# Pairing tiles in PSUM banks and re-ordering the work of an attention-plus-MLP kernel

## The chip, the cores and the metric

The kernel runs on one core of one Trainium2 chip. The metric is the device time of one execution in microseconds (us). The kernel before takes 694.83 us, the median of three runs that lie between 694.37 and 696.42 us.

## The reference

The input `x` has 2048 tokens of 512 numbers. It is normalised token by token, and the result feeds two branches that are added to `x`: causal attention in segments with a compressive memory, and a two-layer MLP. All weights and results are fp32.

```python
x = A_x
xn = _layernorm(x, axis=-1)
return x + _A_ref(xn, A_wq, A_wk, A_wv, A_wo, A_beta) + _B_ref(xn, B_w1, B_b1, B_w2, B_b2)
```

The attention has 32 heads of 16 numbers and 4 segments of 512 tokens. Inside a segment it is an ordinary causal softmax; the memory `M`, `z` carries the earlier segments:

```python
logits = jnp.einsum("bhqd,bhkd->bhqk", qs, ks) * scale + mask
p = _softmax(logits, axis=-1)
a_dot = jnp.einsum("bhqk,bhkd->bhqd", p, vs)
num = jnp.einsum("bhld,bhde->bhle", pq, M)
o = g * a_mem + (1.0 - g) * a_dot
M = M + jnp.einsum("bhld,bhle->bhde", pk, vs)
```

The MLP normalises `xn` again, multiplies by `w1` (512 by 1792), adds a bias, takes a GELU, multiplies by `w2` (1792 by 512) and adds a second bias.

## The kernel before

**Units.** The attention is cut into 16 units, one for each segment and each group of 8 heads. The MLP is cut into 16 units of 256 tokens and 7 of the 14 hidden blocks of 128 (FH = 7).

**Jobs.** The program is a list of small jobs; the letters in quotes are their keys in `streams()` and `CALL`. For TensorE they are of three kinds, by how they use its array of 128 by 128 cells:

- Full array, 128 rows and 128 columns, in `split3` (L480) and `out_jobs` (L815): the query and key projections "T" and the value projection "V" (12 matmuls of 512 columns, since each fp32 product is made of three fp16 products over four slices of 128), the first MLP layer "D" (12 matmuls of 256 columns for one hidden block), and the output projection "out".
- Two halves of 64 rows that work side by side: the maxima "M" (L621), the scores "S" (L661), the second MLP layer "e" (L797, 14 parts of 6 matmuls for one MLP unit), small transposes (L499) and the memory's denominator "Qd" (L571).
- Four column strips of 32 columns side by side, in fp32: the weighted sums of the values "pv" and "PV" (L690, four parts kb = 0 to 3 of 8 instructions each) and the memory update "K" (L602).

**One attention unit.** "T" projects queries and keys, splits them into two fp16 halves and sends them through DRAM into stacked layouts, `kst` and `qst`. "M" multiplies queries by keys for one of four head places t on both halves of the array, and VectorE takes the row maxima under the causal mask (L628). "R" transposes the maxima and sends them through DRAM into two extra rows of `qst`. "S" multiplies the other way round, so that keys lie on partitions and the maximum is already taken off; ScalarE takes the exponential (L666) and GpSimd clears the half above the diagonal (L675). "pv" adds up the values with those weights, for the head places 0 and 2 (half h = 0) and then 1 and 3 (h = 1). "O" divides by the sums.

**The four key blocks.** Causality makes the score strips of key block kb 512, 384, 256 and 128 queries long (`LEN`). For one t, "S" has three jobs: kb 0 (512 columns), kb 1 and 3 together (512) and kb 2 (256). Each job takes two PSUM banks, one for each half of the array, and gives two exponentials. The results lie in a buffer `pt` of 1280 columns, at `OFF`, of which there are 4. "M" has three jobs for one t: query block 3 (512 columns), blocks 2 and 0 (384 and 128) and block 1 (256).

**One MLP unit.** "D" fills 256 columns of a bank for one hidden block, and VectorE scales them into `hz` (L756). "G" takes the seven GELUs on ScalarE (L763), "H" splits the result into two fp16 halves (L770 to L772 on GpSimd and ScalarE), and "e" multiplies by `w2`.

**What sets the order.** Two strings. Each letter of `ORDER` takes the next job of one of 28 streams, and the jobs' instructions go to the five engines in that order; every engine keeps its own order. `BANKS` names the PSUM bank, 0 to 7, for every call of `dense()`, one after the other. Nothing is decided on the chip. The first part of the program also loads, squares ("wm", L311) and splits ("ws", L366 to L371) the six weight matrices; some pieces wait in buffers that later hold other things (`stage`). "warm" is a filler of 8 matmuls.

Of the kernel before, what the change touches and what calls it, by code (L numbers as in the profile page):

```python
# [9 lines left out]
F32 = mybir.dt.float32  # L10
# [9 lines left out]
P = 128  # L20
D = 512
# [25 lines left out]
OFF = [0, 512, 1024, 896]  # L47
# [9 lines left out]
def streams():  # L57
    keys, queries, nat, maxi, soft, vals_p, heads, memo, vals, norm, again, hid, act, mlp, outs, accs, wts = (
        [] for _ in range(17))
    for i in range(NU):  # L60
# [3 lines left out]
        maxi += [("M", i, n) for n in range(12)] + [("R", i)]  # L64
# [17 lines left out]
    for j in range(NU):  # L82
        hf, fh = divmod(j, 2)
        hid += [("D", j, f) for f in range(FH)]
# [18 lines left out]
    "aatcucuccvavtctveecttcetcuvaactvuvtaatcattavdtubcwwvccfwxxcxwxyxyxxgyhxcoxxvwxofooowcvwzyzoiyyiazgyyziiynzoiiys"  # L103
    "ppAnziiniicvzvcniiooAzmAihiiopzqqiqcivpqjpqjijqqijizqjiqqjiiAwszBzoAskkkkmjiAojoijsoAijAqjqjasAfoAopgkkkkpjpjqq"
    "jlpoolojjjooilihAAkkkkpaiqqiqijqjqqijqjiqjqjisBfgpiiqkkkkmpliqqiooiqpBlqoBopohijjiojiijpolsjiqaqajqiqiqqiiqapka"
    "kmkktspaqijqiqjqiqajqbqajopijjgBfopkkkBkjjjlooooBlhjjjolqiqqiipkkkkjiqqijqqjjiqiqjjqiqiqiBkkkkmpliilfnplimpngrr"
    "mrjjponijqjqjinjipiskmkkmkaiijrijjoojiqsjqqjiqiiiqqkkkkihlqlfmlogojqjqjqqjjasoojmkkkkmqjiqjqjjaojjpipmooisikkkk"
    "lpilhiofmgoooqiqpppqiqiqqqiiiqqpsosmoiqqiiqiqppsslooijqjojijojijoiaakkkkmpaijqjqjaqqqjiqqjiqjqiikmkkakbqiaqqahl"
    "olfqjjojqmjgjjoolmmkkkkmhjjoojjiitjiojiippkkkkliiilnfnimpligniinipmrrijjrsijqjqiqjiqjqiipkmkkksiqjqijqjqjiqjqii"
    "qjqikmpkkkiprlqsphlfojmjgopjjlojpjoomokmkkkqiqisjojiqisjqiqijqqijqhiqqiiqjsqiiqppmkkkkilalofomqpgopaoooospmlajq"  # L110
    "qqjqqjqjqiiqiqqqjqiqqipipooooiijooppoiaakkkkmajiqpisqqjiqjqjaiqaqhjqqqjqaaqmkkkkbjlfoljqjmjgojjqolmkkkkmmjjjooj"
    "jioijoiiippkpkkkiinliifniiilnnimlgrpmjjrmjjjrrijikkpskkiqqijqiqijqqjiqjiqjqiqjiqiispqkpkskksqilqoplfojmjgjjjpoo"
    "oojolmkkkkiqjiqpsjiqiqijqjqiqijqjiqiqiqiiqqkksmkpikplolfjjqmjgjjjoooooklpkmkkjiiopjqiqijqjiqpjqiqijqiqqiqiiqikk"
    "pspkkqiplpoooopljjjqqqjqjjqooolkpskmkpkmqqqpqjpjqqqjqjqpqqjqjqqqkmkkkqlllqqqqqqqqqrrrr"
# [5 lines left out]
    "012345670123457063571265407321640573216405732164053271640527163054271630542713605427105472105427105472105472015"  # L120
    "470251407251405712470512470512470536124075631254076340125637123756123576132576132576132576132576135402761350427"
    "163054273106542736574326574326537425632754632574631072456310724563071245360712453620731620731067203617621073621"
    "073621073621037621037621037261702361475023671540263701524603175246031746013746013713460713471630471630463714067"
    "314056723410523674105236741052367410527410527410527410527410527140352671450326475103264751023674523674523647253"
    "647236547236475264735264107532410765324107265431067512043675120436751204736152047361520473615270346150312750317"
    "250317253107250371257013275027135027134650132754062751340621375460376054370567403056374065374065307645307645307"
# [21 lines left out]
def infini_mixer_kernel(ctx: ExitStack, tc: tile.TileContext, x, wq, wk, wv, wo, beta, w1, b1, w2, b2, out):  # L148
# [69 lines left out]
    def col(j):  # L218
        return sc[:, j:j + 1]
# [21 lines left out]

    def four(t):
        return t.rearrange("p (k c) -> p k c", k=KT)

    def w_load(m, k):
        if m in ("qk", "QK"):
            g = 0 if m == "qk" else 1 + k
# [663 lines left out]
```

## Time and profile before

| What | Value |
|---|---|
| Median of three runs | 694.83 us |
| Profiled execution, first to last instruction (span) | 693.1 us |
| Median less span | 1.7 us |
| TensorE clock granted, mean | 0.995 |
| TensorE with a matmul in it | 678.7 us |
| VectorE, ScalarE, GpSimd busy | 535.4, 522.7, 347.2 us |
| Moved by DMA | 55.12 MB |

The profile holds one execution. The profiled execution's own time is its span of 693.1 us; the runs' time also holds what lies around the span, 1.7 us by the difference to the median. PE is TensorE's matmul side and PEld its weight loads, DVE is VectorE, ACT ScalarE, POOL GpSimd and SP the queue that starts the transfers. Lines such as L480 are lines of the kernel before. A group's row gives its busy time in us and the mean length of one instruction in ns; where instructions overlap, busy time over count is less than that mean. A busy PE need not be PE at its peak, because matmuls are pipelined.

### The profile page before, as it was taken

What the parts mean: (1) busy time and instruction counts of PE and PEld (TensorE: products, weight loads), DVE (VectorE), ACT (ScalarE), POOL (GpSimd) and SP (SyncE); (2) the same over time, 40 slices, a digit from 0 to 9 for tenths busy, and PEclk for the clock granted to TensorE, in tenths of its full rate; (3) what the DMA queues carried; (4) which work ended last, traced back from release to release, by engine and by line L of the source; (5) the groups of instructions that cost most, each with busy time, mean ns of one, the idle gap of its engine ahead of it and who ended that gap; (6) DMA issues with size and microseconds to landing.
All of it is one profiled execution on the core that took longest, in us unless ns stands there. A gap on an engine that the chain in (4) does not pass through costs nothing.

```text
span 693.1 us, 16949 instructions
## 1 busy us (share of the span) xinstructions
PE 678.7 (98%) x6359; PEld 395.7 (57%) x6359; DVE 535.4 (77%) x1695; ACT 522.7 (75%) x1013; POOL 347.2 (50%) x533
## 2 busy tenths in 40 slices
PE   7799999999999999999999999999999999999997
PEld 6465556576654555566554456567564456656653
DVE  4499978897795887998798786888678595969442
ACT  5989898878795659857795697757795687778870
POOL 5276768365624425664334445454362546455752
PEclk9899999999999999999999999999999999999999
DMA  9984222420204213431113224231120416140101
GB/s 272 283 238 136 64 63 63 108 62 14 84 10 115 87 44 74 100 71 33 51 45 92 63 72 99 63 93 33 31 80 24 132 18 152 18 108 3 18 1 61
DMA packets 51790, 55.12 MB, mean 80 GB/s; under 512 B 4782, under 2 KB 40636, under 8 KB 51708
## 3 DMA queue, kind: packets, MB, share of 16 engines
q1 hardware_dynamic: 49404, 49.84, 25.3%
q0 software_dynamic: 2304, 4.20, 3.7%
q8 instruction: 50, 0.82, 0.5%
q14 instruction: 32, 0.26, 0.1%
HBM read 36.99 MB, written 17.04 MB: 78 GB/s over the span
## 4 chain that ended last, share of the span: by engine, by line
PE 78%; ACT 10%; POOL 4%; DVE 3%; issue 2%; DMA 1%; SPq 1%; POOLq 0%; ACTq 0%; DVEq 0%
PE ps L480 33%; PE ps L797 16%; PE ps L690 10%; PE ps L815 6%; PE ps L661 5%; PE ps L621 5%; ACT pt L666 2%; DVE ps L628 2%; PE ps L571 2%; PE ps L499 1%; ACT hT L763 1%; ACT hT L771 1%; SPq L252 1%; POOL w1s L371 1%; DMA pt<-in_A_wk_dram 1%
## 5 line engine op out<-in xcount | busy, mean ns | idle before, releaser
L628 DVE CUSTOM_DVE_ANT_0 ps<-ps,mask 128x512 f32<-128x512 f32 (+3 forms) x512 | 233.8, 522 | 16.1 <-PE ps L621 14.9
L666 ACT ACTIVATE pt<-ps,qkcs 128x512 f32<-128x512 f32 (+1 forms) x384 | 206.1, 624 | 35.3 <-PE ps L661 33.5
L797 PE MATMUL ps<-w2s,hT 64*128 64x512 f16 x1344 | 176.7, 376 | 0.2
L480 PE MATMUL ps<-xnT,w1s 128*128 128x256 f16 x1344 | 157.8, 273 | 0.0
L675 POOL TENSOR_SCALAR_AFFINE_SELECT pt<-pt 128x256 f32<-128x256 f32 x256 | 99.1, 414 | 92.0 <-ACT pt L666 91.0
L480 PEld LDWEIGHTS <-w1s 128*128 128x128 f16 x1344 | 127.3, 98 | 29.1 <-issue 11.3
L772 POOL TENSOR_TENSOR hT<-hh,hT 128x512 f16<-128x512 f32 x64 | 67.8, 1059 | 82.8 <-ACT hT L771 81.0
L797 PEld LDWEIGHTS <-hT 64*128 64x128 f16 x1344 | 76.3, 94 | 50.7 <-issue 6.0
L690 PE MATMUL ps<-pt,vt 128*32 128x512 f32 (+3 forms) x1024 | 77.3, 435 | 0.1
L756 DVE SCALAR_TENSOR_TENSOR hT<-ps,sc,sr 128x256 f32<-128x256 f32 x112 | 52.1, 478 | 27.2 <-PE ps L480 27.0
L628 DVE DVE_READ_ACCUMULATOR2_ANT mc<- 128x1 f32 x512 | 70.6, 138 | 0.0
L661 PE MATMUL ps<-qst,kst 50*128 50x512 f16 (+3 forms) x512 | 67.5, 298 | 0.3 <-ACT pt L666 0.2
L621 PE MATMUL ps<-kst,qst 48*128 48x256 f16 (+3 forms) x512 | 67.1, 297 | 0.5
L771 ACT ACTIVATE hT<-hh 128x512 f16<-128x512 f32 x64 | 36.6, 572 | 33.4 <-POOL hh L770 32.9
L690 PEld LDWEIGHTS ps<-pt,vt 128*32 128x32 f32 x1024 | 31.3, 109 | 42.4 <-issue 30.8
L770 POOL TENSOR_SCALAR hh<-hT,sc 128x512 f32<-128x512 f32 x64 | 41.8, 653 | 26.6 <-ACT hT L763 24.9
L720 POOL TENSOR_TENSOR nN<-nN,oT 128x512 f32<-128x512 f32 x16 | 20.3, 1267 | 61.3 <-DVE oT L546 61.3
L763 ACT ACTIVATE hT<-hT,b1t 128x256 f32<-128x256 f32 x112 | 46.4, 495 | 0.2
L480 PE MATMUL ps<-xnT,wqs 128*128 128x512 f16 x192 | 45.6, 389 | 0.0
L480 PE MATMUL ps<-xnT,wks 128*128 128x512 f16 x192 | 44.3, 379 | 0.0
L480 PE MATMUL ps<-wvs,xnT 128*128 128x512 f16 x192 | 44.0, 380 | 0.1
L815 PE MATMUL ps<-wos,oT 128*128 128x512 f16 x192 | 43.2, 380 | 0.6 <-POOL oT L726 0.6
(217 smaller groups left out, 890.0 us busy)
## 6 DMA issues: line engine op xcount, KB each, us to landing
kd<-hl SPq DMA_DIRECT2D x48, 128.0 KB
qd<-hl SPq DMA_DIRECT2D x48, 128.0 KB
kst<-kd SPq DMA_DIRECT2D x32, 192.0 KB
qst<-qd SPq DMA_DIRECT2D x32, 192.0 KB
acc<-in_A_x_dram SPq DMA_DIRECT2D x16, 256.0 KB
acc<-in_B_b_dram POOLq DMA_DIRECT2D x16, 256.0 KB, 4.1
out_dram<-acc SPq DMA_DIRECT2D x16, 256.0 KB
xt<-in_A_x_dram SPq DMA_DIRECT2D x14, 256.0 KB
```

Of the source, the lines that this page charges most:

```text
L480: T.matmul(p, wsl(ws, k, a), xsl(xs, k, b), start=s0 and i == 0, stop=s1 and i == 3 * n - 1)
L621: T.matmul(p[:, o:o + n], stk[i, 0][r, t, P * qb:P * qb + P], stk[i, 1][r, t, :n], start=True, stop=True)
L628: V.tensor_tensor_reduce(p[:, o:o + n], p[:, o:o + n], mask[:, 512 - n:], 1.0, -3e38, OP.add, OP.max, mc[:, 16 * b + 4 * t + qb:16 * b + 4 ...
L661: T.matmul(p[:, o:o + n], stk[i, 1][r, t, P * kb:P * kb + P], stk[i, 0][r, t, P * kb:], start=True, stop=True)
L666: A.activation(e[:, OFF[kbs[0]]:OFF[kbs[0]] + o], p[:, :o], AF.Exp, scale=qkcs[:, 1, i % NG:i % NG + 1])
L675: G.affine_select(v, v, pattern=[[0, 2], [1, P]], compare_op=OP.is_ge, fill=0.0, base=0, channel_multiplier=-1)
L690: T.matmul(p[32 * c:32 * c + 32, P * kb:], vt[s, kb][:, 4 * g + c, 16 * odd:16 * odd + 32], pt[i, 2 * c + odd][:, OFF[kb]:OFF[kb] + LEN[kb ...
L756: V.scalar_tensor_tensor(hz[:, fi, :], p[:, :256], col(F1 + fh), srow[hs][:, own], op0=OP.mult, op1=OP.mult)
L763: A.activation(z, z, AF.Gelu_apprx_tanh, bias=b1t[:, FH * (j % 2) + f:FH * (j % 2) + f + 1])
L772: G.tensor_tensor(hT[:, z, 1, :], t, hT[:, z, 0, :], op=OP.subtract)
L797: w = T.matmul(pes[j][a], hTs[fh][r, fi, u, P * a:P * a + P], w2s[r, fo, v, :], start=n == 0 and m == 0, stop=fi == FH - 1 and m == 2, ski ...
L815: T.matmul(p, o[:, u, P * b:P * b + P], wos[:, g, v, :], start=i == 0, stop=i == 3 * NG - 1)
```

## The change

Four things are changed.

- "D" takes two hidden blocks at a time: they fill the two halves of one bank, and one VectorE instruction of 512 columns scales both. The 7 blocks of an MLP unit become 3 pairs and a single.
- The short maxima, query block 1, of the head places t and t + 1 share a pair of banks; the reductions stay one by one. An attention unit has 10 jobs "M" in place of 12.
- The short scores, kb 2, of the head places h and h + 2 share a pair of banks, with one exponential of 512 columns for each bank. An attention unit has 10 jobs "S" in place of 12. `pt` gives way to three kinds of buffers of 512 columns: 4 of `pa` (kb 0), 4 of `pb` (kb 1 and 3) and 2 of `pc` (kb 2 of two places). The diagonal block of kb 0 is now cleared by an instruction of its own of 128 columns, right after its exponential; kb 1 and 3 together and the two kb 2 have one of 2 by 128 each.
- `ORDER` and `BANKS` are new from end to end. Staged pieces of `wq` and `wk` lie in `pa`, those of `wv` in the second `hT`.

The core of the difference (of the strings one line each):

```diff
-            soft += [("S", i, t, n) for t in ts for n in range(3)]
+            soft += [("S", i, t, n) for t in ts for n in range(2)] + [("S", i, h, 2)]
...
-        hid += [("D", j, f) for f in range(FH)]
+        hid += [("D", j, f) for f in range(0, FH, 2)]
...
-    "aatcucuccvavtctveecttcetcuvaactvuvtaatcattavdtubcwwvccfwxxcxwxyxyxxgyhxcoxxvwxofooowcvwzyzoiyyiazgyyziiynzoiiys"
+    "atacccutatctactuevvetvavvtcvcuatavcaetwuadtwvwuwtvcccvwfxxccxctgcxycxxhwxxycgxvxbosoxywfyyzoyoizyizyizynzynzizA"
...
-        return [f(t, q) for t in range(4) for q in ((3,), (2, 0), (1,))]
+        return [f(t, q) for a in (0, 2) for t, q in (((a,), (3,)), ((a,), (2, 0)), ((a + 1,), (3,)), ((a + 1,), (2, 0)), ((a, a + 1), (1,)))]
...
                 for b, p in enumerate(ps):
-                    e = pt[i, 4 * b + t]
-                    A.activation(e[:, OFF[kbs[0]]:OFF[kbs[0]] + o], p[:, :o], AF.Exp, scale=qkcs[:, 1, i % NG:i % NG + 1])
+                    e = sb.tile([P, 512], F32, name=("pa", "pb", "pc")[kbs[0]], bufs=2 if len(ts) > 1 else 4)
+                    A.activation(e, p, AF.Exp, scale=qkcs[:, 1, i % NG:i % NG + 1])
...
+                for e in es:
+                    if kbs[0] == 2:
+                        v = e.rearrange("p (t c) -> p t c", t=2)[:, :, :P]
+                    elif kbs[0] == 1:
+                        v = e.rearrange("p (a c) -> p a c", c=P)[:, 0:4:3, :]
                     else:
-                        return
-                    G.affine_select(v, v, pattern=[[0, 2], [1, P]], compare_op=OP.is_ge, fill=0.0,
+                        v = e[:, :P].unsqueeze(1)
+                    G.affine_select(v, v, pattern=[[0, v.shape[1]], [1, P]], compare_op=OP.is_ge, fill=0.0,
                                     base=0, channel_multiplier=-1)
...
-                fo = FH * fh + fi
-                p = dense()
-                split3(p[:, :256], ((WT["1"], lambda w, k, a: w[:, fo, a, P * k:P * k + P]),
-                                    (xnT[hs], lambda t, k, a: t[:, k, a, own])), KT, True, True)
-                V.scalar_tensor_tensor(hz[:, fi, :], p[:, :256], col(F1 + fh), srow[hs][:, own], op0=OP.mult, op1=OP.mult)
+                n = min(2, FH - fi)
+                p = dense().rearrange("p (n c) -> p n c", n=2)[:, :n, :]
+                for a in range(n):
+                    fo = FH * fh + fi + a
+                    split3(p[:, a], ((WT["1"], lambda w, k, u: w[:, fo, u, P * k:P * k + P]),
+                                     (xnT[hs], lambda t, k, u: t[:, k, u, own])), KT, True, True)
+                V.scalar_tensor_tensor(hz[:, fi:fi + n, :], p, col(F1 + fh), srow[hs][:, own].unsqueeze(1).broadcast_to([P, n, 256]),
+                                       op0=OP.mult, op1=OP.mult)
```

Three places show what the new order does. In the rows below, a number, the kernel's line, the operation, what it writes and what it reads; `ps_` with a number is one use of a PSUM bank.

On TensorE, at the end of the first layer of MLP unit 3. Before, the last two hidden blocks (here `ps_2217` and `ps_2263`) stand apart, with scores (L661) and maxima (L621) around them:

```order
1866 L621 MATMUL ps_2208<-kst_92,qst_90 128x128
1867 L480 LDWEIGHTS w1s
1868 L480 MATMUL ps_2217<-xnT,w1s 128x256
...
1890 L480 MATMUL ps_2217<-xnT,w1s 128x256
1891 L661 LDWEIGHTS kst_91
1892 L661 MATMUL ps_2231<-qst_89,kst_91 128x256
...
1906 L661 MATMUL ps_2254<-qst_89,kst_91 128x512
1907 L480 LDWEIGHTS w1s
1908 L480 MATMUL ps_2263<-xnT,w1s 128x256
```

Now (L478 is the line that was L480, L658 was L661 and L620 was L621):

```order
1858 L658 MATMUL ps_2207<-qst_89,kst_91 128x512
1859 L478 LDWEIGHTS w1s
1860 L478 MATMUL ps_2222<-xnT,w1s 128x256
...
1906 L478 MATMUL ps_2222<-xnT,w1s 128x256
1907 L478 LDWEIGHTS w1s
1908 L478 MATMUL ps_2248<-xnT,w1s 128x256
...
1930 L478 MATMUL ps_2248<-xnT,w1s 128x256
1931 L620 LDWEIGHTS qst_90
1932 L620 MATMUL ps_2264<-kst_92,qst_90 128x256
```

A pair of blocks (24 matmuls in one bank) and the single one follow each other, and the maxima and scores that stood between them are moved ahead or behind.

On ScalarE, the exponentials of unit 0 for the first half of the heads, t = 0 and then t = 2. Before, from the kb 2 of t = 0 on:

```order
101 L666 ACTIVATE pt<-ps_1080,qkcs 128x256
102 L666 ACTIVATE pt<-ps_1081,qkcs 128x256
103 L666 ACTIVATE pt<-ps_1108,qkcs 128x512
104 L666 ACTIVATE pt<-ps_1109,qkcs 128x512
105 L370 ACTIVATE w1s<-w1s 128x512
106 L666 ACTIVATE pt<-ps_1130,qkcs 128x512
107 L666 ACTIVATE pt<-ps_1131,qkcs 128x512
108 L666 ACTIVATE pt<-ps_1162,qkcs 128x256
109 L666 ACTIVATE pt<-ps_1163,qkcs 128x256
```

Now:

```order
102 L664 ACTIVATE pa<-ps_1060,qkcs 128x512
103 L664 ACTIVATE pa<-ps_1061,qkcs 128x512
104 L856 ACTIVATE be<-bet 128x4
105 L664 ACTIVATE pb<-ps_1102,qkcs 128x512
106 L664 ACTIVATE pb<-ps_1103,qkcs 128x512
107 L664 ACTIVATE pc<-ps_1124,qkcs 128x512
108 L664 ACTIVATE pc<-ps_1125,qkcs 128x512
```

The four short exponentials have become two long ones, which stand behind all the others of this half.

On TensorE near the start, from the key projection of unit 0 (`wks`) to its query projection (`wqs`). Before, the column sums of the weights' squares (L343 and L345, on `am`) stand between the two:

```order
224 L480 MATMUL ps_393<-xnT,wks 128x512
225 L343 MATMUL ps_416<-am,ones 128x1 x2
226 L343 MATMUL ps_431<-am,ones 128x1 x2
227 L345 MATMUL ps_431<-am,ones 128x1
...
229 L480 MATMUL ps_453<-xnT,wqs 128x512
```

Now:

```order
208 L478 MATMUL ps_392<-xnT,wks 128x512
...
210 L833 MATMUL ps_423<-ones 128x256
...
226 L478 MATMUL ps_432<-xnT,wqs 128x512
...
248 L478 MATMUL ps_432<-xnT,wqs 128x512
249 L341 MATMUL ps_459<-am,ones 128x1 x2
250 L343 MATMUL ps_459<-am,ones 128x1
```

The query projection and a filler (L833) now stand ahead of the sums for `w1`.

More of the change, by code (lines that the diff above doesn't have):

```diff
@@ L108 @@
[L108 to L112, printed above, removed]
@@ L122 @@
[L122 to L126, printed above, removed]
@@ L677, in f @@
             return go
-        return {t: [f(t, q) for q in ((0,), (1, 3), (2,))] for t in range(4)}
+        jobs = {t: [f((t,), q) for q in ((0,), (1, 3))] for t in range(4)}
+        for h in range(2):
+            jobs[h].append(f((h, h + 2), (2,)))
+        return jobs
     nd = {}
```

85 lines of the change are left out of this document (44 added, 41 removed).

## The prediction

> **What bounds the kernel now.** I began with the page: what is busy, and which chain ended last.
>
> ```profile
> span 693.1 us, 16949 instructions
> PE 678.7 (98%) x6359; PEld 395.7 (57%) x6359; DVE 535.4 (77%) x1695; ACT 522.7 (75%) x1013; POOL 347.2 (50%) x533
> PE   7799999999999999999999999999999999999997
> PE 78%; ACT 10%; POOL 4%; DVE 3%; issue 2%; DMA 1%; SPq 1%; POOLq 0%; ACTq 0%; DVEq 0%
> ```
>
> TensorE has a matmul in it nearly throughout, and 78% of the chain is TensorE. Next come the busy times by stretch, for where that holds: the stretch, its length, and the busy us of PE, PEld, DVE, ACT and POOL, with instructions in brackets.
>
> ```profile
> 0.00:20.00 20.00, 16.00 (x125) 12.98 (x126) 9.67 (x36) 12.77 (x33) 8.96 (x24) 1.00 0.96 275
> 20.00:40.00 20.00, 15.10 (x88) 9.52 (x87) 10.48 (x33) 19.23 (x37) 8.45 (x9) 0.83 0.81 245
> 40.00:60.00 20.00, 19.97 (x138) 11.46 (x136) 19.70 (x62) 18.53 (x36) 13.29 (x14) 1.00 0.91 266
> 60.00:80.00 20.00, 19.52 (x203) 10.67 (x200) 19.67 (x83) 17.64 (x36) 14.07 (x20) 1.00 0.21 61
> 80.00:560.00 480.00, 479.83 (x4653) 274.36 (x4654) 388.81 (x1233) 359.50 (x702) 232.43 (x363) 1.00 0.25 66
> ```
>
> Until 80 us the weights are being prepared: TensorE is idle for 4.00 + 4.90 + 0.03 + 0.48 = 9.4 us, while ScalarE or VectorE is nearly full. From 80 to 560 us TensorE is idle for 0.17 us of 480, VectorE has 19% free and ScalarE 25%. So there the time is whatever TensorE's stream needs. The change removes no matmul: both programs have the same ones in another order. It can gain only if the stream has room between matmuls, so I read TensorE's timeline piece by piece (start, length, line).
>
> ```profile
> 302.57 0.81 PE L797 MATMUL ps<-w2s,hT 64*128 64x512 f16 x6
> 303.32 2.79 PE L480 MATMUL ps<-xnT,w1s 128*128 128x256 f16 x24
> 306.04 0.39 PE L621 MATMUL ps<-kst,qst 48*128 48x512 f16 x2
> 306.27 0.38 PE L661 MATMUL ps<-qst,kst 50*128 50x512 f16 x2
> 306.49 0.81 PE L797 MATMUL ps<-w2s,hT 64*128 64x512 f16 x6
> 307.14 0.38 PE L661 MATMUL ps<-qst,kst 50*128 50x384 f16 x4
> 307.45 1.48 PE L480 MATMUL ps<-xnT,w1s 128*128 128x256 f16 x12
> 308.87 0.28 PE L661 MATMUL ps<-qst,kst 50*128 50x256 f16 x2
> ```
>
> Take starts, not lengths. From 303.32 to 306.04, 24 full-array matmuls take 2.72 us; from 307.45 to 308.87, 12 take 1.42. The difference, 1.30, is 12 matmuls, so each run carries about 0.12 us more than its matmuls need. The six parts of "e" take 0.65 us (306.49 to 307.14) where another half-array job follows, and 0.75 (302.57 to 303.32) where a full-array job follows. So a turn from full array to halves, or back, costs 0.10 to 0.12 us, and a turn among half-array jobs costs nothing. I take 0.10.
>
> **The change part by part.** *Fewer turns.* I went through TensorE's order of both programs and counted where a full-array row is followed by a half-array row or the reverse: 163 times before, 91 now. The pairs in "D" and longer runs of one kind do this, as the rows at the end of MLP unit 3 show. 72 × 0.10 = 7.2 us less. Of the 72, ten lie in the first 100 us, where ScalarE, not TensorE, sets the pace; they count only because ScalarE is relieved there too, below. Turns to and from the column strips of "pv" and "K" rise from 68 to 74. No row parts their price cleanly; bounds are 0 and twice the nearest one, 0.20, and I take 0.10: 0.6 us more, between 0 and 1.2.
>
> *The other engines.* The groups that change, and the nearest rows for the new shapes:
>
> ```profile
> L666 ACT ACTIVATE pt<-ps,qkcs 128x512 f32<-128x512 f32 x256 | 158.3, 693 | 24.4 <-PE ps L661 24.1
> L675 POOL TENSOR_SCALAR_AFFINE_SELECT pt<-pt 128x256 f32<-128x256 f32 x256 | 99.1, 414 | 92.0 <-ACT pt L666 91.0
> L666 ACT ACTIVATE pt<-ps,qkcs 128x256 f32<-128x256 f32 x128 | 54.3, 485 | 10.8 <-PE ps L661 9.4 <-PE ps L621 0.9
> L756 DVE SCALAR_TENSOR_TENSOR hT<-ps,sc,sr 128x256 f32<-128x256 f32 x112 | 52.1, 478 | 27.2 <-PE ps L480 27.0
> L803 DVE SCALAR_TENSOR_TENSOR acc<-ps,sc,acc 128x512 f32<-128x512 f32 x32 | 22.5, 742 | 7.5 <-PE ps L797 7.4
> L480 PE MATMUL ps<-xnT,w1s 128*128 128x256 f16 x1344 | 157.8, 273 | 0.0
> ```
>
> ```profile
> 4.31 0.29 POOL L181 TENSOR_SCALAR_AFFINE_SELECT mask<-mask 128x128 bf16<-128x128 bf16 x1
> ```
>
> ScalarE: a long exponential keeps it 158.3/256 = 0.618 us, a short one 54.3/128 = 0.424. 128 short ones become 64 long: 54.3 − 39.6 = 14.7 us less, 0.9 in each unit. VectorE: 112 scalings at 52.1/112 = 0.465 become 48 of 512 columns, at 22.5/32 = 0.703 by L803, and 16 single ones: 52.1 − 41.2 = 10.9 us less. GpSimd: 256 selects at 99.1/256 = 0.387 become 192 of these and 128 of 128 columns, which nothing quite like them prices; between half and all of 0.387 they add 0 to 25 us, and by the 0.29 of the mask's select 12. From 80 to 560 us none of this is on the path: TensorE covers it. If GpSimd's extra work fell on its path, it would show in the wait for L675, below. In the first 100 us, two units give ScalarE 1.8 us, more than the ten turns' 1.0, so I let those ten count in full.
>
> *Two tiles in one bank.* The first block of a pair cannot be scaled before the second is done, 1.30 us later. L480's row says that TensorE idles for 0.0 us ahead of "D"; VectorE, for 27.0 us, waits for TensorE. Nothing is queued behind a lack of banks, and the new program uses fewer banks: I take 0. The Trainium skill, PSUM — Partial Sum Buffer, Summary: rules for kernel authors, says to read PSUM while a matmul runs only from another bank; so the later start is certain, and if every one of the 48 pairs passed its 1.30 us on to TensorE, the sum would be 62 us worse. The 0.0 says that it is not passed on now.
>
> *Short scores of two places.* Their exponentials now end the half's row on ScalarE, right before part kb 2 of "pv". The waits now, and a pair of exponentials:
>
> ```profile
> PEld ps L690 <- POOL pt L675: 3.1, 11, 0.5
> PE ps L343 <- ACT w1s L311: 4.5, 2, 3.3
> ```
>
> ```profile
> 72.91 1.26 ACT L666 ACTIVATE pt<-ps,qkcs 128x512 f32<-128x512 f32 x2
> ```
>
> "pv" waited 11 times, 3.1 us in all. The data need 1.26 + 0.41 (L675) = 1.7 us from the last score matmul. Adding up matmuls (at the slots above) between that matmul and part kb 2, I find under 3.0 us of cover at 7 of 32 places before and at 14 now, the least 1.6 and 2.0, on average 2.4 at the 14. Bounds: 0, if the cover holds, and another 3.1. Since none is now under 1.7, I take 0.5.
>
> *Start.* The second wait above is a full stop of TensorE: the sums of `w1`'s squares stood ahead of the query projection, which now goes first. That could save up to 4.5 us; but ScalarE is full (19.23 of 20), and now has about 3 us more of squaring and splitting ahead of the first key projection's results. Bounds −4.5 and +3; I take 0. The staging in other buffers issues the same loads: 0. The order of SP's queue changes with it, in the same bounds.
>
> *End.* The last chain runs from the last "PV" through the division to "out":
>
> ```profile
> 671.15 6.89 PE L797 MATMUL ps<-w2s,hT 64*128 64x512 f16 x60
> 677.97 2.61 PE L815 MATMUL ps<-wos,oT 128*128 128x512 f16 x11
> 681.20 1.04 PE L815 MATMUL ps<-wos,oT 128*128 128x512 f16 x4 [0.63 <-POOL oT L726]
> ```
>
> Ten parts "e" cover it, and 0.63 us is left bare. Now 13 parts stand there, 3 × 0.65 = 1.95 us more cover, but VectorE does the memory's reciprocal behind that "PV" instead of ahead, about 1.4 us. Between −0.6 and 0; I take 0.
>
> *Sum.* −7.2 + 0.6 + 0.5 = −6.1: a span of 693.1 − 6.1 = 687.0. The median stands 694.83 − 693.1 = 1.7 us above the span, so 688.7 us.
>
> **The rivals.** *More is gained* (chance 0.18). TensorE's 4.5 us stop at the start goes without another in its place: 688.7 − 4.5 = 684.2 us. For it speaks the row; against it ScalarE's 19.23.
>
> *Nothing is gained* (0.14). The 0.10 us at a turn is no cost of its own, and what is saved is waited for elsewhere: 694.8 us. For it: TensorE's weight loads are busy for 57% only. Against it: the same 0.10 at each turn, whatever comes next, and 0.17 us idle in 480. The Trainium skill, Perfetto Trace Analysis, Identifying the Most-Contended Engine, calls matmul busy time a poor measure of nearness to the roof and asks for the weight loads' share; by that rule TensorE need not be the bound, and the time stays. The same skill, TensorEngine Tiling, Key Properties, says that a change of tiling mode drains TensorE; by that the turn is TensorE's own, and I hold the gain likelier.
>
> *Slower* (0.09). Part kb 2 of "pv" waits for the paired exponentials. If another job of two (1.26) stands ahead on ScalarE, the data need 3.0 us, and the 14 places with 2.4 lose 0.6 each, 8 us; if two stand ahead, 4.2 us, and they lose 1.8 each, 25 us. Half and half is 16.5 us: 688.7 − 0.5 + 16.5 = 704.7. It decides from (6.1 + 0.5 + 2.1)/14 = 0.6 us at each place. For it: ScalarE is busy three quarters of the time. Against it: today's longest such wait is 0.5.
>
> **How the numbers follow.** My forecast, between about 686 and 691.5 by the bounds of its small terms, has 0.59. A measurement of this kernel tells about 0.3% from no change, 2.1 us: faster is under 692.7, slower over 696.9. Faster: 0.59 + 0.18 = 0.77; no change 0.14; slower 0.09. The range from 684.5 to 694.5 takes in the forecast, most of the first rival and the near half of the second; what it leaves out is some 0.2.
>
> **What would show it.** Right: runs of 24 and 36 matmuls of "D" with 0.10 us at each end, TensorE idle still under 1 us between 80 us and the end of the stage, ScalarE near 508 and VectorE near 525 us busy, GpSimd near 360. Wrong: waits of L690 for the select well over 3 us in all, new waits of TensorE for banks of "D", or 100 us of start with more than 9.4 us idle.

## The result, and the profile after

The changed kernel takes 703.42 us, the median of 4 runs (701.4 to 704.66); the kernel before, beside it, 694.94 (694.37 to 696.42). The ratio is 1.0117, with a 95% interval from 1.0096 to 1.0137: 8.5 us slower. The profiled execution took 704.07 us, with a span of 702.3 against 693.1.

The page after: the span, what is busy, and the chain that ended last by engine.

```profile
span 702.3 us, 16961 instructions
PE 679.0 (97%) x6359; PEld 396.2 (56%) x6359; DVE 529.4 (75%) x1647; ACT 512.6 (73%) x949; POOL 363.4 (52%) x597
PE 56%; DVE 18%; ACT 11%; issue 5%; DMA 5%; POOL 4%; SPq 0%; POOLq 0%; DVEq 0%; ACTq 0%
```

VectorE, ScalarE and GpSimd moved the way that was forecast (to 525, 508 and 360 us) and ended 3 to 5 us above it: VectorE lost 6.0 us where 10.9 were forecast, ScalarE 10.1 of 14.7, and GpSimd gained 16.2 where 12 were. But TensorE's share of the chain fell from 78% to 56%, and VectorE's rose from 3% to 18%. TensorE is still busy for 97% of the span, and yet something else ends last much more often.

The same stretches as before (length, busy us of PE, PEld, DVE, ACT, POOL, then the granted clock and DMA):

```profile
0.00:20.00 20.00, 15.53 (x103) 12.41 (x103) 9.03 (x35) 13.22 (x33) 9.61 (x24) 0.92 0.99 280
20.00:40.00 20.00, 17.23 (x94) 10.27 (x95) 13.04 (x28) 17.61 (x34) 8.29 (x8) 0.83 0.79 233
40.00:60.00 20.00, 19.34 (x140) 12.45 (x139) 17.85 (x45) 15.30 (x32) 12.53 (x13) 1.00 0.77 238
60.00:80.00 20.00, 18.68 (x160) 10.67 (x159) 18.73 (x76) 18.73 (x37) 14.23 (x18) 1.00 0.30 83
80.00:560.00 480.00, 472.57 (x4616) 275.60 (x4614) 379.12 (x1198) 352.19 (x653) 246.08 (x410) 1.00 0.25 66
```

In the first 80 us TensorE is idle for 4.47 + 2.77 + 0.66 + 1.32 = 9.2 us, as before. From 80 to 560 us, where it was idle for 0.17 us, it is now idle for 7.43.

What it waited for, from the waits of PE (line, releaser: us in all, times, longest). Of this kind the trace of before had a single row, 0.2 us.

```profile
PE ps L620 <- DVE mc L627: 1.9, 3, 1.0
PE ps L620 <- DMA qst<-qd: 1.6, 4, 0.6
PE ps L497 <- DVE mc L627: 1.5, 5, 0.7
PE ps L802 <- DVE hT L760: 0.9, 1, 0.9
PE ps L478 <- DVE hT L760: 0.9, 2, 0.7
PE ps L658 <- DVE phq L528: 0.7, 2, 0.4
PE ps L658 <- DVE mc L627: 0.6, 1, 0.6
```

A wait often falls on the weight load ahead of the matmul, so the waits of PEld belong to it:

```profile
PEld L620 <- DMA qst<-qd: 5.3, 8, 1.1
PEld ps L497 <- DVE mc L627: 3.4, 7, 0.8
PEld ps L694 <- POOL pc L676: 2.6, 11, 0.3
PEld ps L694 <- POOL pb L676: 1.2, 5, 0.3
```

Two kinds stand out. VectorE's reductions (`mc`, L627) and scalings (`hT`, L760) hold up TensorE: as the transposes' operands (L497), and as the last readers of a bank that another tile is to get. And the queries' way through DRAM (`qst<-qd`) holds up the maxima. The wait of "pv" (L694) for the selects is 3.8 us against 3.1 before, with 0.3 as its longest.

One place where this can be watched, in the timeline after. Rows that do not bear on it are left out. The first row is four matmuls of a pair of short maxima on PE; L627 reads them.

```profile
237.87 0.39 PE L620 MATMUL ps<-kst,qst 48*128 48x256 f16 x4
238.15 1.02 DVE L558 TENSOR_TENSOR zr<-bd,mst 64x64 f32<-64x64 f32 x4
238.32 1.46 PE L802 MATMUL ps<-w2s,hT 64*128 64x512 f16 x12
239.20 0.43 DVE L627 CUSTOM_DVE_ANT_0 ps<-ps,mask 128x256 f32<-128x256 f32 x1
239.62 0.38 PE L658 MATMUL ps<-qst,kst 50*128 50x384 f16 x4
239.65 0.43 DVE L627 CUSTOM_DVE_ANT_0 ps<-ps,mask 128x256 f32<-128x256 f32 x1
240.00 0.47 DVE L627 CUSTOM_DVE_ANT_0 ps<-ps,mask 128x256 f32<-128x256 f32 x1
240.38 0.47 DVE L627 CUSTOM_DVE_ANT_0 ps<-ps,mask 128x256 f32<-128x256 f32 x1
240.58 0.39 PE L658 MATMUL ps<-qst,kst 50*128 50x512 f16 x2 [0.58 <-DVE mc L627]
```

The maxima are done at 238.26. VectorE is still at something else and comes to them at 239.20. A single short maximum needs two reductions; the pair needs four, one after the other, until 240.85. The scores at 240.58 want the bank that the third reduction leaves, and TensorE stands still for 0.58 us. No engine is overloaded here; the bank comes back late.

**The whole stream.** I gave every matmul of both traces its slot (the distance between starts where nothing disturbs it) and every turn 0.095 us; what is left between two starts is waiting.

| us | before | after |
|---|---|---|
| matmuls at their slots | 645.0 | 645.0 |
| turns | 22.0 | 15.9 |
| waiting, 0 to 80 us | 18.2 | 20.6 |
| waiting, 80 to 640 us | 6.7 | 19.1 |
| waiting, the end | 1.2 | 1.7 |
| span | 693.1 | 702.3 |

The turns brought 6.1 us. The waiting took 15.3. Of that, 9.0 us are matmuls that start within 0.35 us of the release of their tile's bank: such waits came to 7.6 us before and are 16.6 now, 11.6 of it at moments when none of the eight banks was free. The count leans on the slots: with slots that are 1% shorter the growth is 7 us.

### The profile page after: what moved, and what is told of

Its sections match the earlier page's. It is cut to its first block, busy times and chain, and to the rows that moved or that the text cites. A ratio compares the mean times of both kernels' runs of the same rounds, so it can differ in the third digit from the quotient of the medians.

```text
span 702.3 us, 16961 instructions
## 1 busy us (share of the span) xinstructions
PE 679.0 (97%) x6359; PEld 396.2 (56%) x6359; DVE 529.4 (75%) x1647; ACT 512.6 (73%) x949; POOL 363.4 (52%) x597
## 4 chain that ended last, share of the span: by engine, by line
PE 56%; DVE 18%; ACT 11%; issue 5%; DMA 5%; POOL 4%; SPq 0%; POOLq 0%; DVEq 0%; ACTq 0%
PE ps L478 21%; PE ps L802 13%; PE ps L694 7%; DVE ps L627 6%; PE ps L820 5%; PE ps L620 4%; PE ps L658 4%; DMA qst<-qd 2%; DMA qd<-hl 1%; DVE mc L627 1%; ACT hT L768 1%; ACT pb L664 1%; ACT pa L664 1%; DVE hl L516 1%; PE ps L497 1%
## 5 line engine op out<-in xcount | busy, mean ns | idle before, releaser
L627 DVE CUSTOM_DVE_ANT_0 ps<-ps,mask 128x384 f32<-128x384 f32 (+3 forms) x512 | 233.4, 523 | 17.1 <-PE ps L620 15.2
L478 PE MATMUL ps<-xnT,w1s 128*128 128x256 f16 x1344 | 153.4, 273 | 0.8 <-DVE ame L575 0.3
L478 PEld LDWEIGHTS <-w1s 128*128 128x128 f16 x1344 | 130.0, 98 | 24.9 <-issue 7.1
L777 POOL TENSOR_TENSOR hT<-hh,hT 128x512 f16<-128x512 f32 x64 | 66.8, 1043 | 72.3 <-ACT hT L776 72.3
L664 ACT ACTIVATE pa<-ps,qkcs 128x512 f32<-128x512 f32 x128 | 81.2, 690 | 10.4 <-PE ps L658 9.6
L664 ACT ACTIVATE pb<-ps,qkcs 128x512 f32<-128x512 f32 x128 | 81.2, 693 | 8.0 <-PE ps L658 7.7
L627 DVE DVE_READ_ACCUMULATOR2_ANT mc<- 128x1 f32 x512 | 70.9, 139 | 0.2
L620 PE MATMUL ps<-kst,qst 48*128 48x384 f16 (+3 forms) x512 | 65.7, 297 | 4.1 <-DVE mc L627 1.9
L676 POOL TENSOR_SCALAR_AFFINE_SELECT pb<-pb 128x256 f32<-128x256 f32 x128 | 52.8, 428 | 26.4 <-ACT pb L664 26.1
L658 PE MATMUL ps<-qst,kst 50*128 50x384 f16 (+3 forms) x512 | 64.1, 297 | 1.9 <-DVE phq L528 0.7
L676 POOL TENSOR_SCALAR_AFFINE_SELECT pa<-pa 128x128 f32<-128x128 f32 x128 | 38.3, 308 | 51.2 <-ACT pa L664 50.9
L760 DVE SCALAR_TENSOR_TENSOR hT<-ps,sc,sr 128x512 f32<-128x512 f32 x64 | 42.0, 677 | 22.6 <-PE ps L478 22.4
L620 PEld LDWEIGHTS <-qst 48*128 48x128 f16 x512 | 29.2, 94 | 31.3 <-issue 11.0
L478 PE MATMUL ps<-xnT,wqs 128*128 128x512 f16 x192 | 46.6, 395 | 0.2 <-DVE hl L516 0.2
L478 PE MATMUL ps<-wvs,xnT 128*128 128x512 f16 x192 | 43.9, 379 | 1.2 <-DVE hT L760 0.7
L664 ACT ACTIVATE pc<-ps,qkcs 128x512 f32<-128x512 f32 x64 | 40.7, 694 | 5.9 <-PE ps L658 4.0
```

The lines of the kernel that those rows point to most:

```text
L478: T.matmul(p, wsl(ws, k, a), xsl(xs, k, b), start=s0 and i == 0, stop=s1 and i == 3 * n - 1)
L620: T.matmul(p[:, o:o + n], stk[i, 0][r, t, P * qb:P * qb + P], stk[i, 1][r, t, :n], start=True, stop=True)
L627: V.tensor_tensor_reduce(p[:, o:o + n], p[:, o:o + n], mask[:, 512 - n:], 1.0, -3e38, OP.add, OP.max, mc[:, 16 * b + 4 * t + qb:16 * b + 4 ...
L658: T.matmul(p[:, o:o + n], stk[i, 1][r, t, P * kb:P * kb + P], stk[i, 0][r, t, P * kb:], start=True, stop=True)
L664: A.activation(e, p, AF.Exp, scale=qkcs[:, 1, i % NG:i % NG + 1])
L676: G.affine_select(v, v, pattern=[[0, v.shape[1]], [1, P]], compare_op=OP.is_ge, fill=0.0, base=0, channel_multiplier=-1)
```

## The experiments

**The theory.** The gain per turn is real, but TensorE's stream ran at one speed with VectorE and ScalarE, with eight banks between. What the readers of a job need, from the groups of after (line, engine, operation, count, busy us, mean ns):

```profile
L627 DVE CUSTOM_DVE_ANT_0 ps<-ps,mask 128x384 f32<-128x384 f32 (+3 forms) x512 | 233.4, 523 | 17.1 <-PE ps L620 15.2
L664 ACT ACTIVATE pa<-ps,qkcs 128x512 f32<-128x512 f32 x128 | 81.2, 690 | 10.4 <-PE ps L658 9.6
```

There are 160 jobs of maxima, so each keeps VectorE for 233.4/160 = 1.46 us; a job of scores keeps ScalarE for 2 × 81.2/128 = 1.27. TensorE is done with either in 0.22. Fewer turns mean longer bunches of such jobs; pairs mean banks that are held longer. Both make the readers late and the banks scarce. **The rivals:** the turns have no price of their own; the new order or the new choice of banks is bad as such; the pairs are bad in themselves. The experiments stand by question, not in the order of time; each was timed beside the kernel before, which took 694.87 to 695.41 us.

**What a turn costs.** The kernel before with 50 turns more: at 25 places a job of scores or maxima that followed a block of "D" is put between its matmuls, after the sixth of twelve. Its readers' instructions stay where they were.

```diff
-    def split3(p, parts, n, s0, s1):
+    def split3(p, parts, n, s0, s1, mid=None):
...
+            if k == 2 and mid:
+                mid()
```

> The kernel before with 50 more turns and nothing else: at 25 places where a score or maxima job follows a hidden block D and half-array work comes next, its matmuls stand in the middle of D's twelve; VectorE and ScalarE keep their order. If a turn costs 0.10 us of TensorE, 694.9 + 50 x 0.10 = 699.9 us. If a turn has no price of its own, 694.9 us.

It took 700.14 us, ratio 1.0075 [1.0062, 1.0087]: 5.27 us for 50 turns, 0.105 each. The price that the prediction read from starts is confirmed, and the rival "nothing is gained, because a turn costs nothing" falls.

**The pairs without the new order.** All edits of the code, but `ORDER` and `BANKS` of before, each pair at its second member's place (151 turns).

```diff
-    "atacccutatctactuevvetvavvtcvcuatavcaetwuadtwvwuwtvcccvwfxxccxctgcxycxxhwxxycgxvxbosoxywfyyzoyoizyizyizynzynzizA"
+    "aatcucuccvavtctveecttcetcuvaactvuvtaatcattavdtubcwwvccfwxxcxwxyxyxxgyhxcxxvwxofowcvwzyzoiyyiazgyyziiynzoiiysppAn"
```

> The order and the banks of the kernel before, with the changed tiles: each pair of D, of short maxima and of short scores stands where its second member stood and takes that member's banks. 151 turns between full-array and half-array jobs in place of 165. Theory 1 (the new order costs the time, the pairs cost nothing): 694.9 - 14 x 0.10 = 693.5 us. Theory 2 (the pairs cost it, since their banks are evicted later and their exponentials come together): the 15 us of new waiting stay, 693.5 + 15 = 708 us.

It took 727.05 us, ratio 1.0461 [1.0447, 1.0475], 32 us more than before, with twelve turns fewer, and more than either theory said. From 80 to 560 us:

```profile
80.00:560.00 480.00, 463.24 (x4504) 264.30 (x4504) 368.30 (x1154) 339.80 (x629) 232.25 (x394) 1.00 0.24 61
```

TensorE is idle for 16.8 us there. Waits for a bank come to 34.7 us by the same count as above, and for 28 to 29 of them another bank was free: the choice of banks was made for single tiles.

**Which pairs.** The same with only one kind of pair each, the other left as before.

```diff
-        hid += [("D", j, f) for f in range(FH)]
+        hid += [("D", j, f) for f in range(0, FH, 2)]
```

> The order of before with only the blocks of the first MLP layer in pairs, each pair at its second member's place; scores and maxima single. 151 turns. Playing the order through with durations of the traces gives 709 us. Theory A (each kind of pair holds banks longer and bunches VectorE's or ScalarE's work, and the two add up): 705 to 713 us, about half of the 32 us of all pairs. Theory B (only one kind does the harm): this one at 693 to 697 us and the one with scores and maxima near 727, or the reverse.

```diff
-        maxi += [("M", i, n) for n in range(12)] + [("R", i)]
+        maxi += [("M", i, n) for n in range(10)] + [("R", i)]
...
-            soft += [("S", i, t, n) for t in ts for n in range(3)]
+            soft += [("S", i, t, n) for t in ts for n in range(2)] + [("S", i, h, 2)]
```

> The order of before with only the short scores and short maxima in pairs and the smaller buffers for exponentials; the blocks of the first MLP layer single. 163 turns, as before. Playing the order through gives 711 us. Theory A: 705 to 715 us. Theory B: near 695 or near 727. Since this kernel has not one turn less, whatever it is above 695 is the price of the pairs alone.

"D" alone took 711.64 us (ratio 1.0236 [1.0221, 1.0251]), scores and maxima alone 714.41 (1.0272 [1.0255, 1.0289]). That is 16.4 and 19.2 us, together 35.6 where both at once cost 32: each kind does harm, and they nearly add up. With the gain of twelve turns taken off, the 48 pairs of "D" cost 16.4 + 1.3 = 17.7 us here, 0.37 us for each.

**The choice of banks.** The old order with pairs, with only `BANKS` chosen again: the order was played through on paper with durations from the two traces, and each tile was given the bank that comes free first.

```diff
-    "012345670123457063571265407214573216573216405327164271630527163054273642710547054271054721472015470214072405712"
+    "012345670123457063571526407351240673512406735124067352401637524016375240163740164037410637401634706143761043761"
```

> As old_order_pairs, with the banks chosen anew: each use takes the bank that comes free first when the durations of the two traces are played through this order (2% added to VectorE's and ScalarE's). In old_order_pairs TensorE waits 33 us for banks, 28 of them while another bank is free. Theory A (the pairs are harmless, the old bank string does not fit them): 727 - 28 = 699 us or less. Theory B (pairs in an order made for single tiles bunch the work of VectorE and ScalarE whichever banks they have): about 713 to 716 us by the same play-through.

It took 714.75 us, ratio 1.0281 [1.0265, 1.0298]. 12.3 of the 32 us were the choice of banks; 20 are not. Waits for banks are now 16.5 us, 13.5 of it with none free. In the other direction, the changed kernel's order with each tile on the bank that has been free longest:

> The changed kernel with other banks: every use takes the bank that has been free longest in the order of the program. If the choice of banks makes the waits of scores and maxima for banks (about 5 us of the new waiting by my count of the trace), the time falls to about 698 us. If the order makes them, since VectorE and ScalarE are behind whichever bank is taken, it stays within 1 us of 703.4.

It took 719.58 us, ratio 1.0347 [1.0332, 1.0363]. So the new list of banks is worth 16 us against this one. For 5.0 of the 16.6 us of waits for banks in the changed kernel another bank was free; a list that won all of that back would still leave it slower than before, at about 698 us.

**The new order without the pairs.** The jobs in the order of after, but the tiles of before, both members of a pair at its place:

> The order of the changed kernel with the tiles of the kernel before: each pair is undone in its place into two jobs in a row, the first on a bank that has long been free. 93 turns, as in the changed kernel. Theory 1 (order): the waits stay, about 703 us. Theory 2 (pairs): the turns are saved and nothing is waited for, 694.9 - 7.2 + 0.6 = 688 us.

It took 844.59 us, ratio 1.2143 [1.2124, 1.2161]; it also holds the long buffers `pt` until "PV", and for most of its waits for banks another bank was free, so it parts little. Only "D" undone, two banks for each former pair, everything else as after:

```diff
-        hid += [("D", j, f) for f in range(0, FH, 2)]
+        hid += [("D", j, f) for f in range(FH)]
```

> The changed kernel with the pairs of D alone undone, each in its place: two single blocks in a row on two banks, each scaled as soon as it is done; the other tiles, the order and their banks are as in the changed kernel. If the later eviction of a paired D costs the time (the term I took at 0), it falls well under 703, to 690 or so. If the order does, it stays at 703 or rises by what 48 more uses of banks cost.

It took 766.08 us, ratio 1.1018 [1.1002, 1.1035], with 66.8 us of waiting for banks. For about 50 of these another bank was free when the wait began: it is in good part the list of banks, with an entry put in for each added tile, that does not fit. So these two runs do not part the new order from the pairs: what a pair of "D" costs or saves in the new order is not shown.

**Less work for the readers.** The test that the theory asks for: the same stream of TensorE, but VectorE and ScalarE with less to do. The maxima are taken over half of the columns, without the right mask, and the exponentials over half of theirs, which "pv" then reads twice. With the exponentials halved the result is another one; all matmuls, tiles and orders stay.

```diff
-                        V.tensor_tensor_reduce(p[:, o:o + n], p[:, o:o + n], mask[:, 512 - n:], 1.0, -3e38,
+                        V.tensor_tensor_reduce(p[:, o:o + n // 2], p[:, o:o + n // 2], mask[:, :n // 2], 1.0, -3e38,
...
-                    A.activation(e, p, AF.Exp, scale=qkcs[:, 1, i % NG:i % NG + 1])
+                    A.activation(e[:, :256], p[:, :256], AF.Exp, scale=qkcs[:, 1, i % NG:i % NG + 1])
```

First the maxima alone, in the changed kernel:

> The changed kernel with every row maximum taken over half of its columns, without the mask (the result is wrong by that): the same instructions in the same order, but VectorE has about 512 x 0.17 = 85 us less to do. Theory 1 (the new waits of TensorE are VectorE's and ScalarE's arrears, which the new order makes larger: a maximum starts 1.35 us after its last matmul on average, before 0.99): about half or more of the 15 us go, 703.4 - 9 = 694 us or less. Rival (the waits are those of transfers through DRAM and of a shortage of banks, whatever the pace of VectorE): within 2 us of 703.4.

695.03 us, ratio 1.0001 [0.9988, 1.0014]: as fast as before, 8.4 us gained. Then both, in the changed kernel and in the kernel before:

> As after_half_max, and each exponential of scores covers half of its columns too (the weighted sums read that half twice, so TensorE's work is the same): ScalarE has about 320 x 0.22 = 70 us less as well. Theory 1: nearly all of the new waits go between 80 and 560 us, and what is left is TensorE's own stream with its 93 turns: 693.1 - 7.2 + 0.6 + 1.7 = 688 us or a little less. Rival: within 2 us of 703.4.

> The kernel before with half maxima and half exponentials (the short exponentials in full). Control for the two runs above: TensorE waits for nothing between 80 and 560 us there, so the relief can only act at the start and the end: 692 to 694.9 us. If the turns are worth their price, the changed kernel with the same relief lies about 6 us under this one; if they are worth nothing, it lies at the same time.

They took 690.04 (ratio 0.9927 [0.9912, 0.9941]) and 690.53 (0.9934 [0.9917, 0.995]). The relief brings the changed kernel 13.4 us and the kernel before 4.4, and the difference of 8.5 us between the two kernels is gone. It is not quite the same relief: ScalarE's busy time falls by 62.2 us in the changed kernel and by 48.5 in the kernel before, where the short exponentials stay whole; VectorE's by 75.9 and 71.7. A fuller relief could bring the kernel before little more, since its waits for banks are down to about 3 us. So of the other 9.0 us at least about 6 are what the change had put on VectorE and ScalarE. The changed kernel was expected 6 us under the kernel before here, and is level with it. In the relieved pair the turns' gain can be seen as well. The page of before with the relief, and that of after:

```profile
PE 675.4 (98%) x6359; PEld 383.2 (56%) x6359; DVE 463.7 (67%) x1695; ACT 474.2 (69%) x1013; POOL 347.3 (50%) x533
```

```profile
PE 669.6 (97%) x6359; PEld 383.1 (56%) x6359; DVE 453.5 (66%) x1647; ACT 450.4 (65%) x949; POOL 361.4 (52%) x597
```

PE is busy for 5.8 us less with the same matmuls, and still the spans are equal, 688.8 us each: what the turns save is waited for elsewhere. With the relief, after still waits for the queries' way through DRAM (a row of PE and one of PEld). The stretch from 80 to 560 us, of the relieved before and then of the relieved after, shows that the waits lie there: TensorE is idle for 0.46 and 4.02 us. Up to 80 us it is idle for 8.2 and 8.8 us, so the start differs little.

```profile
PE ps L620 <- DMA qst<-qd: 2.8, 3, 1.3
```

```profile
PEld L620 <- DMA qst<-qd: 5.1, 7, 1.6
```

```profile
80.00:560.00 480.00, 479.54 (x4675) 267.06 (x4674) 334.95 (x1240) 324.34 (x705) 233.48 (x366) 1.00 0.25 66
```

```profile
80.00:560.00 480.00, 475.98 (x4716) 270.84 (x4712) 327.68 (x1218) 312.45 (x665) 249.59 (x421) 1.00 0.25 67
```

**Is it the pair or the reader?** The relief in the old order with pairs, with the old banks and with the new ones:

> The order and banks of before with all the pairs (727.05 us), and with the row maxima and the exponentials over half of their columns: the other half of the scores is not used, so the result is another one. Theory A (the loss is VectorE's and ScalarE's arrears, which hold the banks): with half the work there are no arrears, and what is left is the kernel before with the same relief, 690.5 us, less 12 turns of 0.105, so 689 to 694 us. Theory B (a pair's bank is held longer because its second member is multiplied later, whatever VectorE and ScalarE do): most of the 32 us stay, over 705 us.

> The order of before with all the pairs and with banks chosen anew for them (714.75 us), with the row maxima and the exponentials over half of their columns: the other half of the scores is not used, so the result is another one. Theory A (what stayed at 707 us in the same order with the old banks is that those banks were dealt out for single tiles, and what goes with half the work is arrears): with new banks and half the work both are gone, 688 to 694 us. Theory B (a pair holds its bank too long wherever it stands): well over 695, about 700 us.

| us | full work | half the maxima and exponentials | relief |
|---|---|---|---|
| before | 694.9 | 690.5 | 4.4 |
| its order with pairs, banks of before | 727.05 | 707.05 | 20.0 |
| its order with pairs, banks chosen again | 714.75 | 698.99 | 15.8 |
| after | 703.42 | 690.04 | 13.4 |

Neither theory has it alone. Late readers are about 15.6 of the old order's 32 us (20.0 − 4.4, with the relief as unequal as above). The banks' choice is 8.1 us even with the relief. And 8.5 us stay (698.99 against 690.53). A block of "D" and others of its line hold their bank for 4.5 us on average there (3.5 in the relieved before), so a pair may cost by itself in an order that was made for single tiles. That is not shown: of some 8 us of waits for banks in this run, about 5 fall where another bank was free, and the list had been chosen with the full durations. In the changed kernel's order, with the relief, the pairs are level with the single tiles.

**Trying to mend it.** Two ways. First, the changed kernel with the first maxima of units 3, 9, 11, 12 and 14, which wait for `qst`, put 1.3 to 2.7 us later in the stream, and banks chosen again:

```diff
-    "maiprnptiiirrppsrijqqijqisqjqjqijpqimkkkkijqqijqjqijqqjhqippkkmkkllfojjmlgjmjjoookmkkppkiqiqjiqqpsiqijqqiqhqijq"
+    "maiprnptiriirppsrijqqijqisqjqjqijpqimkkkkijqqijqjqijqqjhqippkkmkkllfojjmlgjmjjoookmkkppkiqiqjiqqpsiqijqqiqhqijq"
```

> The changed kernel with the first maxima of units 3, 9, 11, 12 and 14 moved behind 1.3 to 2.7 us of other TensorE work, so that 11.5 us or more lie between the later projection and the first maxima (9.0 to 10.5 in the changed kernel); banks chosen anew by the play-through. If the waits at these five places (6.2 us by my count) are the way of the queries through DRAM and nothing takes their place: 703.4 - 5 = 698 us. If they only move the arrears on, to later waits for banks: 702 to 703 us.

706.88 us, ratio 1.0165 [1.0152, 1.0178]: slower still. The waits moved on to the banks, 20.7 us now, 18.1 with none free. Second, orders and banks from a search that plays the program through with the traces' durations, with pairs (145 turns) and with the tiles of before (174 turns):

> The tiles of the changed kernel in a third order with its own banks, searched with the durations of the two traces, 2% added to VectorE's and ScalarE's and 30% to the transfers' way: 145 turns in place of 93, but scores and maxima spread so that VectorE and ScalarE keep up (0.2 us of waits for banks by the play-through). Theory 1 (the changed kernel loses by its order, not by its pairs): 681.1 + 1.7 = 683 us, up to 688. Rival (the pairs cost it): not under 695.

> The tiles of the kernel before, single, in an order and banks searched in the same way, 174 turns. 684.1 + 1.7 = 686 us if the play-through holds. Against planned_pairs it shows what the pairs are worth when both orders are made with the same care: 3 us by the play-through, 0 if they are worth nothing.

702.25 us (ratio 1.0102 [1.0087, 1.0116]) and 698.26 (1.0046 [1.0033, 1.0059]): both missed, by 19 and 12 us, though the same play-through gave 709 and 711 us for the two kernels with one kind of pair (711.64 and 714.41). A searched order may use up every margin that the durations on paper leave; no run shows that this is the cause. The two also answer what the pairs are worth when both orders are searched with the same care: the kernel with pairs has 29 turns fewer and is 4.0 us slower. With the relief:

> The order with pairs and banks that was searched by play-through (702.25 us, where 683 had been expected), with the row maxima and the exponentials over half of their columns: the other half of the scores is not used, so the result is another one. Theory A (its 19 us of excess are arrears of VectorE and ScalarE that the play-through does not show, since it uses one duration for each kind): 686 to 690 us, since it has 145 turns against the 163 of before, which with the same relief takes 690.5 us. Theory B (the excess is something else: transfers, the start, the clock): 693 us or more.

696.3 us, ratio 1.0023 [1.0011, 1.0036]: a relief of 6.0 us, little more than the 4.4 of before. So the excess of this order is not what the late maxima and exponentials were in the changed kernel. Part of it is one row of PE's waits in the run without the relief, for the maxima's way through DRAM:

```profile
PE ps L658 <- DMA qst<-md: 3.4, 3, 2.6
```

The rest stays open. No version that does the whole work was faster than the kernel before.

## Why the prediction was wrong, point by point

- **From 80 to 560 us the time is whatever TensorE's stream needs.** True of before, but the idle time of 0.17 us does not show the margin. Between 80 and 640 us, 134 of the 1008 tiles of before started within 0.25 us of the release of their bank. VectorE and ScalarE were not on the path, and were just behind it.
- **Fewer turns, −7.2 us.** Right in mechanism and nearly in size: 0.105 us each in the kernel with 50 more, −6.1 by the account of the stream, 5.8 us less busy time in the relieved pair.
- **The other engines' busy time.** Right in direction, 3 to 5 us too low: 529.4, 512.6 and 363.4 us. That "none of this is on the path: TensorE covers it" was wrong. Totals fell, and yet the readers came later. From a tile's last matmul to the start of its reader, between 80 and 640 us, it was 0.99 us on average for the maxima, 0.81 for the scores and 0.73 for "D" and its line before; it is 1.35, 1.08 and 1.35 now. The totals cannot do this; bunches and pairs can.
- **Two tiles in one bank, 0 us.** This is the step that failed, together with "TensorE covers it": the sum put at nothing the waits for a bank that a late reader still holds. The reason given was L480's 0.0 us of idle time and "Nothing is queued behind a lack of banks". Waits for banks went from 7.6 to 16.6 us. In the order of before the pairs of "D" alone cost 16.4 us, those of scores and maxima 19.2. There are fewer tiles now, but each holds its bank longer: one of "D" and its line 5.6 us on average against 3.6, so that 5.06 of 8 banks are held at once on average against 4.91. The bound of 62 us was too wide, the 0 not justified. How much of the loss in the new order belongs to the pairs and how much to the bunches that the order makes is not shown.
- **Part kb 2 of "pv", +0.5 us.** Right: 3.8 us of waits against 3.1. The rival that ended on the slower side named this place; the time came near its 704.7, but by another mechanism.
- **Start, 0 us.** The 4.5 us stop for `w1s` shrank, as the first rival hoped, and another took its place, as ScalarE's full row said (waits of PE):

```profile
PE ps L324 <- ACT wqs L309: 2.9, 1, 2.9
PE ps L341 <- ACT w1s L309: 2.3, 2, 1.4
```

  TensorE's waiting by the account of the stream still grew by 2.4 us; longer stretches at half the clock, 10.2 us in place of 6.8, are the likely reason. It was not tried alone, but in the relieved pair, with 6.8 us at half the clock in each, the starts are nearly level.
- **End, 0 us.** Right: the last chain is bare for 0.53 us against 0.63.

```profile
690.33 8.16 PE L820 MATMUL ps<-wos,oT 128*128 128x512 f16 x37 [0.53 <-POOL oT L730]
```

So 8.5 us slower is 6 us of turns gained, about 9 lost to readers that hold banks longer and come later, and some 6 to the queries' and maxima's way through DRAM and the start. At least 6 of the 9 are shown by the relief; the parting of the other 6 is read from the trace alone, and the run that was to win back the queries' way through DRAM did not. The Trainium skill, Perfetto Trace Analysis, Identifying the Most-Contended Engine, had been set against the turns' gain, in the rival that nothing is gained: matmul busy time as a poor measure of nearness to the roof. The turns were TensorE's own, and still the rule's warning held in this case: at 98% busy, the engine was not the only bound.

## What to carry to other kernels

An engine that is busy all the time shows that it is kept fed, not by how much: before work is bunched, count how many buffers are taken again within a quarter of a microsecond of their release, and what each job costs its reader against its writer (here 1.3 to 1.5 us against 0.22). Tiles that share a bank, the order and the choice of banks are one decision; a saving of 0.1 us at a turn is worth having only where the bunch that it makes fits into the banks that are free. To learn whether readers are the cause, halve their work and leave the stream as it is, by the same amount in both kernels: the difference between the two that goes with it is theirs.

## What the runs showed of the hardware

**TensorE's clock falls to half after short stops.** Windows of the changed kernel from 10 to 37 us (the granted clock is the third number from the end):

```profile
10.00:13.30 3.30, 2.25 (x21) 1.92 (x18) 0.00 (x0) 2.93 (x7) 3.13 (x6) 1.00 1.15 306
13.30:16.70 3.40, 1.59 (x14) 1.50 (x15) 1.19 (x4) 3.34 (x12) 3.13 (x10) 1.00 1.08 350
16.70:20.10 3.40, 3.28 (x17) 2.39 (x15) 3.34 (x14) 3.40 (x7) 1.96 (x3) 0.50 1.18 292
...
26.90:30.30 3.40, 1.33 (x7) 0.51 (x5) 1.94 (x4) 3.37 (x5) 0.00 (x0) 1.00 0.57 120
30.30:33.70 3.40, 3.21 (x16) 2.02 (x17) 1.39 (x6) 3.06 (x10) 0.69 (x1) 0.51 0.86 295
33.70:37.10 3.40, 3.40 (x9) 1.29 (x8) 2.22 (x2) 2.78 (x7) 2.26 (x2) 0.50 1.15 301
```

After a stop of 2.9 us (12.24 to 15.11) the clock is 0.50 for 3.4 us, in which PE is busy for 3.28; after stops of 0.82 and 1.44 close together it is half for 6.8 us. The kernel before has one such stretch, from 24.7 to 31.5 us, which begins within a stop of 3.31 us; stops of 1.31 and 1.00 us there, from 8.29 and 11.75 us, left the clock at 1.00. The kernel with "D" undone in the new order, with 39.6 us of idle TensorE from 80 to 560 us, had a mean clock of 0.969. The Trainium skill, TensorE: Matmul & The Clock Gate, What's actually happening, puts the idle window at about 3.4 us; here stops that are shorter were enough, and the length of a stretch at half the clock agrees.

**A VectorE instruction can take three times its length beside GpSimd.** One operation on SBUF alone, of 128 by 512, in the changed kernel (shortest, median, longest in ns), and one of its long cases in the timeline:

```profile
L527 DVE TENSOR_SCALAR phk<-phk,qksc x12: 471/481/1399, 27.7 to 457.9; 128x512 f32<-128x512 f32 x12
```

```profile
262.24 1.26 POOL L581 TENSOR_TENSOR ame<-ame,rc 128x512 f32<-128x512 f32 x1 [3.57 <-DVE rc L544]
262.68 1.11 DVE L527 TENSOR_SCALAR phq<-phq,qksc 128x512 f32<-128x512 f32 x1
```

It takes 0.48 us mostly. Of the 24 of this line (12 on `phk`, 12 on `phq`), ten took 0.65 us or more, up to 1.40. Each of the ten started while a GpSimd TENSOR_TENSOR was running, and ended 0.28 us after that one's end (here 263.50 and 263.79); two beside which a TENSOR_TENSOR began only after their own start took 0.48. No run moves GpSimd's work alone, so that GpSimd is the cause was not tried by itself. It is one way in which a plan with one duration for each kind of instruction can come out late.
